# A fused attention and expert-routing kernel: a third buffer of token rows, another order of loads, and weight pieces held back at the seam

## The chip, the cores and the metric

One Trainium2 chip, one of its NeuronCores. The metric is the device time of one execution of the whole program in microseconds (us). TensorE (PE in the rows) multiplies matrices, VectorE (DVE) and ScalarE (ACT) work on elements, GpSimd (POOL) does some elementwise work and issues DMAs from its own queue, and SyncE (SP) only issues DMAs. The 16 DMA engines of the core serve both queues.

## What is computed

Linear attention with decay over blocks of 64 positions, and then a mixture of eight experts on its output, one expert per token:

```python
for b in range(nb):                                  # q, k, v: 4 batches, 8 heads, 768 positions, 64 wide, fp32
    intra = einsum('bhij,bhjd->bhid', (qb @ kb.T) * Dmask, vb)
    inter = einsum('bhid,bhde->bhie', qb * lam_pow, kv_state)
    out[:, :, sl] = intra + inter
    kv_state = lam_block * kv_state + einsum('bhsd,bhse->bhde', kb * rev_pow, vb)
x = out as 3072 rows (tokens) of 512
logits = normalised(x) @ normalised(expert_emb).T / tau      # 8 experts
e = argmax(logits); gate = softmax(logits)[e]
out[token] = gate * (max(x[token] @ w1[e], 0) @ w2[e])       # w1: 512x1024, w2: 1024x512 per expert, fp32 in memory
```

## The kernel before, in words

**Attention.** The 3072 tokens are 24 tiles of 128, six to a batch. The loop `for i in range(-2, R)` is a software pipeline with the order of every engine written out by hand: slot i loads k and v for tiles ahead (`load_k`, `load_v`, 256 KB each) and q for a pair of tiles ahead (`load_q`, 512 KB), transposes q and k of tile i + 2 (`pe_Tq` L302, `pe_Tk` L315), routes tile i - 1 (`pe_X`, L403), forms the scores of tile i + 1 (`pe_ST`, L327) and the output of tile i (`pe_O`, L363). ACT copies a pair of q into `qr` (`act_q`, L284), and `pe_Tq` waits for that. Pool scales k into `ks` (`pool_ks`). All q, k and v loads stand in SP's queue in program order, and a load waits there until its buffer is free: `qn` has 2, `kn` 4, `vn` 6.

**Routing.** `pe_X` leaves each token's row in `xg` (fp16 values, the token's number and its gate). Tiles are routed in groups: four groups of four tiles, four groups of two. The first tile of a group takes an `xg` buffer (`tensor_copy` L400 on DVE, with z, the scores and all later DVE work behind it); a buffer is free when all `scatter`s (L524, Pool) of the group that had it before have landed. Groups of four have 2 buffers, groups of two have 3. `scatter` writes a tile's rows to the expert's area of `xs_dram`; `at(i, "pool", ...)` fixes the slots, and `late` spreads a group's scatters over slots. Slots for weight pieces ("w") are a list of tile numbers. Pool's DMAs take turns on eight semaphores, and each waits until the DMA eight before it has landed.

**The seam.** Rows of an expert's area come in two parts: tiles below `TA` fill rows from 0, later tiles go on at row `CA` = 256 at the earliest (`bump`). So rows 0 to 255 of the first three experts (`NA`) can be read early (`load_early`): a one-element read `mark` of `xs_dram` (L552) waits for all scatters so far, and the three reads ("a", L546) follow it on SP. Scatters that come later in the program wait for `mark`, since it reads what they write. `early_xT` transposes the first of these row blocks in an attention slot. `fill` writes rows that are never used with an out-of-range number. After the loop come the last tile's routing, its two scatters, then the reads of the remaining rows: three "b" (L546), four small ones for the joint remainder (`x_q`, L565), and all 384 rows of expert 3 ("f", L546). PE meanwhile runs both layers (`pe_L1` L747, `pe_L2` L779) for the early rows A[0] to A[2], then B_[0] to B_[2], then experts 3 to 7 (F_[3] to F_[7]).

**Weights.** Each expert has four pieces (two of w1, two of w2), 512 KB each after the cast to fp16. `load_w` issues the next piece from Pool. Twelve go out in attention, two after it, and the other 18 behind the output writes: `put` (L760, L763) scales a block of output on DVE, writes it by an indirect DMA from Pool, and then issues `more.get(n_scat, 1)` pieces. Once, before F_[3], DVE waits for a Pool instruction that stands behind such a `put`: `overs` has Pool write `pstart` (an iota, L799), DVE computes `below` from it, and the copy `add_q` (L729) that completes F_[3]'s rows stands behind that on DVE.

Of the kernel before, what the change touches and what calls it, by code (L numbers as in the profile page):

```python
# [22 lines left out]
def kernel(  # L23
# [19 lines left out]
    R = B * RB  # L43
# [12 lines left out]


    NA = 3
    TA = 18
    CA, CE, GE = 256, 416, 3  # L60
    CQ = CE - GE * P
    NQ = P // CQ
# [49 lines left out]
    def load_q(j):  # L112

        if not 0 <= j < NJ:
            return
        b, c = divmod(2 * j, RB)
        qn[j] = ring.tile([P, H, 2, D], FP32, name="qn", tag="qn", bufs=2)
        nc.sync.dma_start(qn[j], q[b, :, ds(c * P, 2 * P), :].rearrange("h (p s) d -> p h s d", s=2))
# [8 lines left out]
    def load_v(i):  # L127
        if not 0 <= i < R:
            return
        b, c = divmod(i, RB)  # L130
        vn[i] = ring.tile([P, H, D], FP32, name="vn", tag="vn", bufs=6)
        nc.sync.dma_start(vn[i], v[b, :, ds(c * P, P), :].rearrange("h p d -> p h d"))

    load_k(0)
    load_q(0)
    load_k(1)
    load_v(0)
    nc.sync.dma_start(emb_sb, moe_expert_emb)
    load_k(2)
    load_q(1)  # L140
    load_k(3)
    load_v(1)

# [55 lines left out]
    nsq_all = const.tile([P, R], FP32, name="nsq_all")  # L199
    z_sb = const.tile([P, 2, 4, E], FP32, name="z_sb")  # L200
    ohcum = const.tile([P, E], FP16, name="ohcum")
    GZ = 6
    zrow = wk.tile([P, GZ, DM2], I32, name="zrow", tag="zrow", bufs=1)
    row_a = const.tile([P, 2], FP32, name="row_a")
    row_b = const.tile([P, 1], FP32, name="row_b")
# [186 lines left out]
    def xT_of(i, a):  # L392
        return xT[i][:, a // 2, a % 2, :]

    def pe_X(t):
        gi, j = group_of[t]
        if j == 0:
            nt = len(groups[gi])
            xg[gi] = xgp.tile([P, nt, DM2], I32, name="xg", tag=f"xg{nt}", bufs=2 if nt == 4 else 3)
            nc.vector.tensor_copy(xg[gi][:, 0:nt, DW : DW + 1],  # L400
                                  tok_iota[:, groups[gi][0] : groups[gi][0] + nt].unsqueeze(2))
        for a in range(DC):
            nc.tensor.matmul(xz[:, a // 2, a % 2, :], xT_of(t, a), ien[:, a, :], start=(a % 2 == 0),  # L403
                             stop=True, skip_group_check=True)
# [125 lines left out]

    def fill():

        p = P // 8
        rows = xs_dram.rearrange("(e r) d -> e r d", e=E)[:, CE - GZ * p : CE, :]
        nc.sync.dma_start(rows.rearrange("e (p g) d -> p e (g d)", p=p),
                          zrow[0:p].rearrange("p g d -> p (g d)").unsqueeze(1)
                          .to_broadcast([p, E, GZ * DM2]))


    xe, xi, xTe, xq, hT, hq = {}, {}, {}, {}, {}, {}  # L540
# [59 lines left out]
    def at(i, slot, fn, *a):  # L600
        todo.setdefault((i, slot), []).append((fn, a))
# [5 lines left out]
    for gi in range(GL):  # L607
        n = groups[gi][-1] + 1
        at(n, "z", rt_a, gi)
        at(n, "end", rt_n, gi)  # L610
        at(n + 1, "dve", rt_a2, gi)
        if groups[gi][0] == TA:
            at(n + 1, "pe", pe_part)
            at(n + 2, "dve", rt_part)
        at(n + 1, "pe", pe_rank, gi)
        if n + 2 < R:
            at(n + 2, "dve", rt_b, gi)
            at(n + 2, "z", rt_c, gi)
            at(n + 2, "end", rt_d, gi)
        else:  # L620
            at(n + 1, "pe", rt_b, gi)
            at(n + 1, "pe", rt_c, gi)
            at(n + 1, "mid", rt_d, gi)
            for j in range(2):
                at(n + 1, "mid", scatter, gi, j)
        if n + 2 < R:
            for j in range(len(groups[gi])):
                late = 0 if n >= TA else (j + 1) // 2 if n > TA - 4 else j
                at(min(n + 2 + late, R - 1), "pool", scatter, gi, j)
    at(0, "sp", fill)  # L630
    at(21, "sp", load_early)
    for i in (8, 11, 14, 16, 17, 18, 18, 19, 19, 22, 22, 22):
        at(i, "w", load_w, 1)

    def early_xT():
        xt_copy(("a", 0), 0, 2, ps.tile([P, DC * 2 * P], FP16, name="q_xtr", tag="q"))

    at(R - 1, "pe3", early_xT)

    act_q(0)  # L640
    pool_ks(0)
    for i in range(-2, R):
        if i >= -1:
            load_k(i + 5)
            load_v(i + 3 if i < 2 else i + 4)
            if i == 1:
                load_v(5)
            if i % 2 == 0:
                load_q(i // 2 + 2)
        run(i, "sp")  # L650
        pe_Tq(i + 2)
        pe_Tk(i + 2)
# [47 lines left out]
    ntile = const.tile([P, E], I32, name="ntile")  # L700
    pstart = const.tile([P, R], FP32, name="pstart")
    n_scat = [0]
    more = {2: 2, 3: 2, 9: 0, 10: 0, 11: 2, 12: 2}

    with (
        tc.tile_pool(name="wpool2", bufs=3) as wpool2,
# [47 lines left out]
        def put(y_ps, key, g):  # L754
# [14 lines left out]
                oob_is_err=False,  # L769
            )  # L770

            load_w(more.get(n_scat[0], 1))
            n_scat[0] += 1

        def pe_L2(key, g):
# [35 lines left out]

        A, B_, F_ = ([(k, e) for e in range(E)] for k in "abf")
        load_w(2)
        pe_X(R - 1)
        rt_a(GL)
        rt_a2(GL)
        rt_n(GL)
        pe_L1(A[0], range(4))
        pe_rank(GL)
        rt_b(GL)  # L820
        rt_c(GL)
# [149 lines left out]
```

## Time and profile before

| | |
|---|---|
| time, median of 3 runs | 285.45 us (284.69 to 287.54) |
| the profiled execution: time, span | 287.21 us, 285.3 us |
| busy share of the span: PE, DVE, ACT, POOL | 82%, 43%, 45%, 35% |
| mean granted TensorE clock | 0.924 of full |
| the chain that ended last: PE, DMA, issue, DVE, ACT | 44%, 20%, 11%, 8%, 8% |
| read from and written to HBM | 55.88 MB, 10.78 MB |

The span runs from the first to the last instruction; 1.9 us of the profiled execution lie around it. The share of the chain is what the last-ending sequence of waits and work was made of, and it changes along the span, so the stages are read apart.

### The profile page before, as it was taken

The page shows a single profiled execution, that of the slowest core. Times are in us where ns is not written, and L with a number is a line of the kernel's source. Part 1 is how long each engine was busy: PE and PEld are TensorE (multiplying, and loading weights), DVE is VectorE, ACT ScalarE, POOL GpSimd, SP SyncE. Part 2 cuts the span into 40 slices and gives each one's busy share as a digit, 9 for nine tenths or more (in the row PEclk, how much of TensorE's full clock was granted, in tenths as well). Part 3 has the DMA queues.
Part 4 walks back from the last instruction along what each step waited for, and adds up shares of the span by engine and source line. Part 5 has one row for each costly group of instructions (what it writes and reads, how often), then busy time and mean ns, then how long its engine had stood idle before and what let it go on. Part 6 is the DMA issues. An engine that isn't in the chain of part 4 may idle for free.

```text
span 285.3 us, 7195 instructions
## 1 busy us (share of the span) xinstructions
PE 233.3 (82%) x2926; PEld 176.3 (62%) x2926; DVE 123.6 (43%) x413; ACT 127.6 (45%) x282; POOL 101.1 (35%) x142
## 2 busy tenths in 40 slices
PE   0899669998399769989898797539949999999970
PEld 0688558887388658978777575216725465555520
DVE  1265325655445255676966322014531534334340
ACT  5765334662436155556435654004614353643500
POOL 4651211075009303905625655022420355132150
PEclk9999969999779979999999999658987999999995
DMA  7999989689709976997976999999982179960220
GB/s 159 237 243 150 208 200 197 140 212 191 184 22 196 202 177 137 206 211 154 215 159 157 178 241 268 251 268 285 196 162 40 65 168 230 256 195 38 77 106 18
DMA packets 72558, 49.93 MB, mean 175 GB/s; under 512 B 52024, under 2 KB 64952, under 8 KB 72515
## 3 DMA queue, kind: packets, MB, share of 16 engines
q0 software_dynamic: 7840, 26.25, 41.9%
q1 hardware_dynamic: 64674, 23.13, 36.3%
q8 instruction: 25, 0.41, 0.6%
q14 instruction: 19, 0.15, 0.2%
HBM read 55.88 MB, written 10.78 MB: 234 GB/s over the span
## 4 chain that ended last, share of the span: by engine, by line
PE 44%; DMA 20%; issue 11%; DVE 8%; ACT 8%; POOL 4%; SPq 2%; POOLq 1%; ACTq 0%; DVEq 0%
DMA xs_dram<-xg,si 9%; PE h_ps L747 7%; DMA qn<-in_q_dram 7%; PE s_ps L327 6%; PE y_ps L779 6%; PE o_ps L363 5%; PE xps L403 5%; DMA x_q<-xs_dram 5%; PE q_ps L302 4%; POOL out_dram L763 3%; PE o_ps L380 3%; PE k_ps L315 3%; PE o_ps L354 2%; ACT qr L284 2%; ACT xT L369 2%
## 5 line engine op out<-in xcount | busy, mean ns | idle before, releaser
L747 PE MATMUL h_ps<-xTe,w_sb 128*128 128x416 f16 (+2 forms) x352 | 51.4, 303 | 6.0 <-DVE xTe L729 3.8
L749 ACT ACTIVATE hT<-h_ps 128x384 f16<-128x384 f32 (+2 forms) x88 | 34.8, 402 | 41.4 <-PE h_ps L747 40.4
L763 POOL DMA_INDIRECT out_dram<-y_sb,xi x26 | 26.1, 1002 | 76.2 <-DVE y_sb L760 46.3
L747 PEld LDWEIGHTS <-w_sb 128*128 128x128 f16 x352 | 36.5, 116 | 21.1 <-issue 10.8
L524 POOL DMA_INDIRECT xs_dram<-xg,si x24 | 24.5, 1020 | 66.6 <-ACT kT L317 22.5
L779 PE MATMUL y_ps<-w_sb,hT 128*128 128x512 f16 x192 | 47.7, 400 | 0.0
L302 PE MATMUL q_ps<-ident,qr 128*128 128x128 f32 x96 | 18.0, 317 | 23.1 <-ACT qr L284 23.1
L290 POOL TENSOR_TENSOR ks<-kn,kdec 128x512 f32<-128x512 f32 x24 | 25.3, 1055 | 30.9 <-DMA kn<-in_k_dram 12.4
L336 DVE TENSOR_TENSOR stm<-s_ps,step 64x512 f32<-64x512 f32 (+1 forms) x48 | 30.7, 676 | 12.9 <-PE s_ps L327 12.9
L760 DVE TENSOR_SCALAR y_sb<-y_ps,x_e 128x512 f32<-128x512 f32 x24 | 18.0, 750 | 41.6 <-PE y_ps L779 39.1
L779 PEld LDWEIGHTS <-hT 128*128 128x128 f16 x192 | 18.9, 102 | 20.6 <-issue 3.3
L408 ACT ACTIVATE sq<-xps 128x512 f16<-128x512 f32 x24 | 14.3, 597 | 36.6 <-DVE z_sb L405 29.6
L403 PE MATMUL xps<-ien,xT 128*128 128x136 f32 x192 | 29.0, 298 | 1.6 <-ACT xT L369 1.6
L327 PE MATMUL s_ps<-qT,kT 64*64 64x64 f32 (+1 forms) x768 | 28.7, 270 | 1.2 <-DVE qT L304 0.8
L302 PEld LDWEIGHTS q_ps<-ident,qr 128*128 128x128 f32 x96 | 11.6, 157 | 27.6 <-ACT qr L284 17.0
L403 PEld LDWEIGHTS xps<-ien,xT 128*128 128x128 f32 x192 | 26.4, 207 | 2.4 <-ACT xT L369 2.2
L327 PEld LDWEIGHTS s_ps<-qT,kT 64*64 64x64 f32 x768 | 22.6, 143 | 5.2 <-DVE qT L304 2.4
L363 PE MATMUL o_ps<-stm,vn 128*64 128x128 f32 x384 | 25.3, 274 | 0.0
L751 DVE TENSOR_SCALAR hq<-h_ps 128x32 f16<-128x32 f32 x64 | 12.2, 191 | 27.2 <-ACT hT L749 26.1
L369 ACT COPY xT<-o_ps 128x512 f32<-128x512 f32 x24 | 14.0, 585 | 19.1 <-PE o_ps L363 19.0
L363 PEld LDWEIGHTS o_ps<-stm,vn 128*64 128x64 f32 x384 | 20.6, 137 | 0.7 <-issue 0.7
L304 DVE TENSOR_TENSOR qT<-q_ps,lamq 128x512 f32<-128x512 f32 x24 | 16.3, 679 | 9.9 <-PE q_ps L302 9.9
(126 smaller groups left out, 267.6 us busy)
## 6 DMA issues: line engine op xcount, KB each, us to landing
w_sb<-in_moe_w_dram POOLq DMA_DIRECT2D x32, 512.0 KB, 9.5
kn<-in_k_dram SPq DMA_DIRECT2D x24, 256.0 KB, 5.7
qn<-in_q_dram SPq DMA_DIRECT2D x12, 512.0 KB, 5.6
vn<-in_v_dram SPq DMA_DIRECT2D x24, 256.0 KB, 5.6
x_e<-xs_dram SPq DMA_DIRECT2D x5, 387.0 KB, 14.9
xs_dram<-zrow SPq DMA_DIRECT2D x1, 774.0 KB
x_e<-xs_dram SPq DMA_DIRECT2D x3, 258.0 KB, 3.1
out_dram<-y_sb,xi POOLq DMA_INDIRECT x26, 3.1
```

What stands on the lines that cost most here:

```text
L290: nc.gpsimd.tensor_tensor(ks[i], kn[i], kdec[:, i % RB].unsqueeze(2).to_broadcast([P, H, D]), op=ALU.mult)
L302: nc.tensor.transpose(t[:, hp, :], qr[j][:, s, 2 * hp : 2 * hp + 2, :].rearrange("p h d -> p (h d)"), ident)
L327: nc.tensor.matmul(sb[ds(C * c, C), h2, hp, c:2, :], kT[i][ds(64 * h2, 64), hp, ds(C * c, C)], q_of(i, hp, c)[ds(64 * h2, 64)], start=(hp ...
L336: nc.vector.tensor_tensor(stm[i][0:n, :, :, c], sb[0:n, :, :, c], step[0:n, c].rearrange("p s i -> p (s i)").unsqueeze(1).unsqueeze(1) .to ...
L363: nc.tensor.matmul(o_at(h2, u, b2), vn[i][:, 2 * hp + h2, :], stm[i][:, h2, hp], start=(i % RB == 0 and b2 == 0), stop=True, skip_group_ch ...
L369: nc.scalar.copy(xT[i].rearrange("p b h t -> p h b t"), bank["o"][:, :, 0 : 2 * P].rearrange("p h (b t) -> p h b t", t=P))
L403: nc.tensor.matmul(xz[:, a // 2, a % 2, :], xT_of(t, a), ien[:, a, :], start=(a % 2 == 0), stop=True, skip_group_check=True)
L524: nc.gpsimd.indirect_dma_start(out=xs_views[groups[gi][j]], out_offset=bass.IndirectOffsetOnAxis(ap=slot_i[gi][:, j : j + 1], axis=0), in_ ...
L747: nc.tensor.matmul(h_ps[:, 0:n], w_cols(w, c, fc), xTe[key][:, c, 0:n], start=(c == 0), stop=(c == DC - 1))
L749: nc.scalar.activation(hT[key][:, fc, 0:nm], h_ps[:, 0:nm], AF.Relu)
L763: nc.gpsimd.indirect_dma_start(out=out_views[n_scat[0]], out_offset=bass.IndirectOffsetOnAxis(ap=xi[key][:, g : g + 1], axis=0), in_=y[:], ...
L779: nc.tensor.matmul(y_ps, hT[key][:, fc, ds(P * g, P)], w[:, fc, :], start=(fc == 0), stop=(fc == FC - 1))
```

## The change

Eight edits. Groups of four tiles get a third `xg` buffer. `vn` goes from 6 buffers to 5, v is asked at i + 3 throughout, and q at pair i/2 + 3 in place of i/2 + 2 (pair 1 and pair 2 move up accordingly at the start). `TA` goes from 18 to 16, with `load_early` in slot 20 in place of 21, `early_xT` in slot 22 in place of 23, and the scatters of the fourth group in pairs. `fill` writes 627 KB in two DMAs instead of 774 KB in one. The pieces in attention move to other slots. After the loop no piece goes out behind the first output write; behind the second, Pool copies one element of expert 3's rows into `seen`, so it waits for that read, and issues four pieces; the following counts are redistributed (18 as before). ACT's cast of the last tile's rows (`x_cast`) moves behind the first chunk of A[0]'s first layer.

```diff
-    TA = 18
+    TA = 16
-        vn[i] = ring.tile([P, H, D], FP32, name="vn", tag="vn", bufs=6)
+        vn[i] = ring.tile([P, H, D], FP32, name="vn", tag="vn", bufs=5)
...
     load_k(1)
-    load_v(0)
+    load_q(1)
     nc.sync.dma_start(emb_sb, moe_expert_emb)
     load_k(2)
-    load_q(1)
+    load_v(0)
...
-            xg[gi] = xgp.tile([P, nt, DM2], I32, name="xg", tag=f"xg{nt}", bufs=2 if nt == 4 else 3)
+            xg[gi] = xgp.tile([P, nt, DM2], I32, name="xg", tag=f"xg{nt}", bufs=3)
...
+        for ne, p, end in ((NA, P // GZ // 4, CA), (E, P // GZ // 2, CE)):
+            rows = xs_dram.rearrange("(e r) d -> e r d", e=E)[0:ne, end - GZ * p : end, :]
...
-                late = 0 if n >= TA else (j + 1) // 2 if n > TA - 4 else j
+                late = 0 if n > TA else j // 2 if n == TA else j
     at(0, "sp", fill)
-    at(21, "sp", load_early)
-    for i in (8, 11, 14, 16, 17, 18, 18, 19, 19, 22, 22, 22):
+    at(20, "sp", load_early)
+    for i in (8, 10, 12, 14, 15, 16, 17, 20, 20, 21, 21, 22):
         at(i, "w", load_w, 1)
...
-    at(R - 1, "pe3", early_xT)
+    at(R - 2, "pe3", early_xT)
...
+            if i == -1:
+                load_q(2)
             load_k(i + 5)
-            load_v(i + 3 if i < 2 else i + 4)
-            if i == 1:
-                load_v(5)
+            load_v(i + 3)
             if i % 2 == 0:
-                load_q(i // 2 + 2)
+                load_q(i // 2 + 3)
...
-    more = {2: 2, 3: 2, 9: 0, 10: 0, 11: 2, 12: 2}
+    more = {1: 4, 2: 1, 3: 1, 4: 2, 5: 2, 6: 1, 7: 1, 8: 1, 9: 1, 11: 2, 12: 2}
...
-            load_w(more.get(n_scat[0], 1))
+            if n_scat[0] == 1:
+                nc.gpsimd.tensor_copy(seen, xe["f", NA][0:1, 0, DW : DW + 1])
+            load_w(more.get(n_scat[0], 0))
...
-        pe_X(R - 1)
+        pe_X(R - 1, cast=False)
         rt_a(GL)
         rt_a2(GL)
+        pe_L1(A[0], range(1))
+        x_cast(R - 1)
+        pe_L1(A[0], range(1, 2))
         rt_n(GL)
-        pe_L1(A[0], range(4))
+        pe_L1(A[0], range(2, 4))
```

On SP, from the v load of tile 2 to the q load of pair 3 (qn_428), before:

```order
L132 DMA vn_271<-in_v_dram 128x8x64
L118 DMA qn_273<-in_q_dram 128x8x128
L535 DMA xs_dram_78<-zrow_161 16x8x1548
L125 DMA kn_344<-in_k_dram 128x8x64
L132 DMA vn_346<-in_v_dram 128x8x64
L132 DMA vn_348<-in_v_dram 128x8x64
L125 DMA kn_424<-in_k_dram 128x8x64
L132 DMA vn_426<-in_v_dram 128x8x64
L118 DMA qn_428<-in_q_dram 128x8x128
```

On SP now, from the q load of pair 2 (qn_195) to `fill`, with pair 3 as qn_275:

```order
L118 DMA qn_195<-in_q_dram 128x8x128
L125 DMA kn_197<-in_k_dram 128x8x64
L132 DMA vn_199<-in_v_dram 128x8x64
L125 DMA kn_271<-in_k_dram 128x8x64
L132 DMA vn_273<-in_v_dram 128x8x64
L118 DMA qn_275<-in_q_dram 128x8x128
L540 DMA xs_dram_78<-zrow_161 8x3x1032
L540 DMA xs_dram_78<-zrow_161 16x8x1032
```

The q load of pair 3 moved from behind `fill` and five loads of k and v to just ahead of `fill`, with the third and fourth v load now behind it or close to it.

On Pool near the end of attention, before, from the scatter of tile 15 to those of tiles 20 and 21 (xg_1706 holds tiles 16 and 17, xg_1887 tiles 18 and 19):

```order
L524 DMA xs_dram_78<-xg_1354,si_1792 24576x258
L524 DMA xs_dram_78<-xg_1706,si_1976 24576x258 x2
L524 DMA xs_dram_78<-xg_1887,si_2155 24576x258 x2
L276 DMA w1_sb_1954<-in_moe_w1_dram 128x2048
L276 DMA w2_sb_1955<-in_moe_w2_dram 128x2048 x2
L524 DMA xs_dram_78<-xg_2085,si_2263 24576x258 x2
```

On Pool now, from the scatters of tiles 16 and 17 (xg_1711, the first that wait for `mark`) to those of tiles 18 and 19:

```order
L529 DMA xs_dram_78<-xg_1711,si_1987 24576x258 x2
L276 DMA w2_sb_1599<-in_moe_w2_dram 128x2048
L276 DMA w1_sb_2068<-in_moe_w1_dram 128x2048 x2
L276 DMA w2_sb_2069<-in_moe_w2_dram 128x2048
L529 DMA xs_dram_78<-xg_1887,si_2158 24576x258 x2
```

The first scatters behind `mark` were those of tiles 18 and 19 and are now those of tiles 16 and 17, with four weight pieces queued between them and the next scatters.

On Pool after the loop, before, from the last two pieces that go out without an output write to the second output write (y_sb_2489):

```order
L276 DMA w1_sb_2335<-in_moe_w1_dram 128x2048 x2
L524 DMA xs_dram_78<-xg_2243,si_2395 24576x258 x2
L763 DMA out_0_dram<-y_sb_2472,xi_2470 3072x512
L276 DMA w2_sb_2336<-in_moe_w2_dram 128x2048
L763 DMA out_0_dram<-y_sb_2489,xi_2470 3072x512
```

On Pool now, from the last tile's scatters to the third output write (y_sb_2575) and a piece behind it:

```order
L529 DMA xs_dram_78<-xg_2255,si_2397 24576x258 x2
L769 DMA out_0_dram<-y_sb_2474,xi_2472 3072x512
L769 DMA out_0_dram<-y_sb_2490,xi_2472 3072x512
L779 COPY seen_2318<-x_e_2448 1x1
L276 DMA w2_sb_2338<-in_moe_w2_dram 128x2048 x2
L276 DMA w1_sb_2498<-in_moe_w1_dram 128x2048 x2
L769 DMA out_0_dram<-y_sb_2575,xi_2573 3072x512
L276 DMA w2_sb_2499<-in_moe_w2_dram 128x2048
```

The pieces behind the first two output writes moved behind the copy that waits for expert 3's rows, and all later output writes and pieces stand behind that wait too.

## Rows read from the trace of the kernel before

**Rows 1.** Chain that ended last, in order of time: start us, us, what.

```profile
30.25 6.93 DMA qn<-in_q_dram
...
163.49 10.54 DMA xs_dram<-xg,si
...
197.11 1.74 PE y_ps L779 x8
```

**Rows 2.** Timeline of PE, output matmuls of tiles: start us, us, what.

```profile
32.19 1.05 PE L363 MATMUL o_ps<-stm,vn 128*64 128x128 f32 x16
...
44.95 1.05 PE L363 MATMUL o_ps<-stm,vn 128*64 128x128 f32 x16
...
64.24 1.05 PE L363 MATMUL o_ps<-stm,vn 128*64 128x128 f32 x16
...
70.47 1.04 PE L363 MATMUL o_ps<-stm,vn 128*64 128x128 f32 x16
...
82.52 1.05 PE L363 MATMUL o_ps<-stm,vn 128*64 128x128 f32 x16
...
96.84 1.05 PE L363 MATMUL o_ps<-stm,vn 128*64 128x128 f32 x16
...
107.90 1.04 PE L363 MATMUL o_ps<-stm,vn 128*64 128x128 f32 x16
...
153.25 1.09 PE L363 MATMUL o_ps<-stm,vn 128*64 128x128 f32 x16
```

**Rows 3.** Timeline, DVE taking an `xg` buffer; in brackets idle time and what ended it.

```profile
73.44 0.17 DVE L400 COPY xg<-tok_iota 128x4 int32<-128x4 int32 x1 [4.35 <-DMA xs_dram<-xg,si]
...
100.14 0.17 DVE L400 COPY xg<-tok_iota 128x4 int32<-128x4 int32 x1 [5.08 <-DMA xs_dram<-xg,si]
```

**Rows 4.** Windows: length, busy PE, PEld, DVE, ACT, POOL, then clock, DMA share, GB/s.

```profile
32.00:153.00 121.00, 102.39 (x1800) 90.64 (x1798) 67.33 (x216) 55.78 (x125) 42.22 (x45) 0.93 0.82 178
...
229.00:256.00 27.00, 27.00 (x161) 15.90 (x159) 9.88 (x33) 13.40 (x25) 11.08 (x15) 1.00 0.93 221
...
45.00:65.00 20.00, 19.92 (x376) 17.70 (x373) 12.51 (x38) 11.67 (x25) 6.96 (x7) 1.00 0.78 178
66.00:76.00 10.00, 4.74 (x97) 3.94 (x96) 4.43 (x10) 3.09 (x8) 2.16 (x3) 0.94 0.96 199
```

**Rows 5.** DMA issues of the page: KB each, median us to landing.

```profile
qn<-in_q_dram SPq DMA_DIRECT2D x12, 512.0 KB, 5.6
...
xs_dram<-xg,si POOLq DMA_INDIRECT x24, 5.7
```

**Rows 6.** Timeline, Pool, SP and DVE at the seam.

```profile
149.38 0.26 SPq L552 DMA_DIRECT2D mark<-xs_dram  x1
...
152.38 0.16 DVE L400 COPY xg<-tok_iota 128x2 int32<-128x2 int32 x1
...
159.06 1.16 POOL L276 DMA_DIRECT2D w_sb<-in_moe_w_dram  x2
...
167.63 0.58 POOL L276 DMA_DIRECT2D w_sb<-in_moe_w_dram  x1 [1.01 <-DMA w_sb<-in_moe_w_dram]
...
177.62 17.61 SPq L546 DMA_DIRECT2D x_e<-xs_dram  x4
```

**Rows 7.** Timeline of PE and Pool from A[2]'s first layer to F_[5]'s.

```profile
173.07 3.66 PE L747 MATMUL h_ps<-xTe,w_sb 128*128 128x256 f16 x32
...
181.44 0.61 PE L593 MATMUL xtr<-ident,x_e 128*128 128x128 f16 x4 [4.71 <-DMA x_e<-xs_dram]
...
193.88 3.01 PE L747 MATMUL h_ps<-xTe,w_sb 128*128 128x160 f16 x32
...
210.95 0.20 POOL L799 IOTA pstart<- 128x24 f32 x1
...
212.39 8.60 PE L747 MATMUL h_ps<-xTe,w_sb 128*128 128x416 f16 x32 [3.84 <-DVE xTe L729]
...
251.79 5.79 PE L747 MATMUL h_ps<-xTe,w_sb 128*128 128x416 f16 x32
```

More of the change, by code (lines that the diff above doesn't have):

```diff
@@ L201 @@
     ohcum = const.tile([P, E], FP16, name="ohcum")
-    GZ = 6
+    GZ = 4
     zrow = wk.tile([P, GZ, DM2], I32, name="zrow", tag="zrow", bufs=1)
@@ L393, in xT_of, with pe_X @@
         return xT[i][:, a // 2, a % 2, :]
-    def pe_X(t):
+    def pe_X(t, cast=True):
         gi, j = group_of[t]
@@ L408, in pe_X, with x_cast @@
         nc.scalar.activation(sq, xz[:, :, :, 0:P], AF.Square, accum_out=nsq_all[:, t : t + 1])
+        if cast:
+            x_cast(t)
+    def x_cast(t):
+        gi, j = group_of[t]
         nc.scalar.copy(
@@ L531, in fill @@
     def fill():
[L533 to L537, printed above, removed]
+        for ne, p, end in ((NA, P // GZ // 4, CA), (E, P // GZ // 2, CE)):
+            rows = xs_dram.rearrange("(e r) d -> e r d", e=E)[0:ne, end - GZ * p : end, :]
+            nc.sync.dma_start(rows.rearrange("e (p g) d -> p e (g d)", p=p),
+                              zrow[0:p].rearrange("p g d -> p (g d)").unsqueeze(1)
+                              .to_broadcast([p, ne, GZ * DM2]))
     xe, xi, xTe, xq, hT, hq = {}, {}, {}, {}, {}, {}
@@ L702 @@
     n_scat = [0]
-    more = {2: 2, 3: 2, 9: 0, 10: 0, 11: 2, 12: 2}
+    more = {1: 4, 2: 1, 3: 1, 4: 2, 5: 2, 6: 1, 7: 1, 8: 1, 9: 1, 11: 2, 12: 2}
+    seen = const.tile([1, 1], I32, name="seen")
     with (
```

## The prediction, on record before the changed kernel ran

> **What bounds the kernel now.** I read the chain that ended last first, in order of time, for its long DMA pieces. Three of those matter here: a q load in early attention (6.93 us), and at the seam a scatter that took 10.54 us to land [rows 1]. The timeline of PE then gives the pace. Undisturbed, four tiles take 64.24 - 44.95 = 19.29 us, so 4.82 each; at that pace the 20 steps from tile 3 to tile 23 would take 96.4, and they took 121.1 [rows 2]. Three steps hold most of the loss: tile 3 to 4 took 12.76 (7.9 too long), 9 to 10 took 12.05 (7.2), and 13 to 14 took 11.06 (6.2) [rows 2]. The first is the q load of pair 3, issued at 30.25 and landed at 37.18, when tile 4 should already have been at work [rows 1, 2]. The other two are DVE waiting, in front of all its later work, for an `xg` buffer whose last scatter had not landed [rows 3]. These losses include the stretch after each wait in which PE's granted clock was down (0.93 on average over 32 to 153 us, against 1.00 in an undisturbed stretch) [rows 4].
>
> After attention PE has the early rows of three experts to work on, up to 173.07 + 3.66 = 176.73. It then waits for the b rows and `x_q` and reaches B_[0]'s first layer only at 193.88 [rows 7]. What it waits for began with the last scatter: issued at 163.49, landed at 174.03 [rows 1], behind weight pieces in Pool's queue [rows 6]; the reads then share the DMA engines with more pieces. From there on PE waits once more, 3.84 us in front of F_[3] [rows 7], and is busy all of the time in the stretch that follows [rows 4].
>
> **The q load.** Pair 3 is now asked before `fill` and before five loads that stood in front of it. It and all that stands ahead of it are 4.7 MB; at the 178 GB/s of attention [rows 4] that is 26.5 us from the start. ACT wants it one tile ahead of tile 4, at about 32.2 [rows 2]. I count the whole 7.9. For later pairs the request comes four tiles (19.3 us) ahead of its use, against a median landing of 5.6 [rows 5]. v is asked when the same buffer comes free as before (tile i - 2, since both the depth and the buffers fell by one), still over four tiles ahead, so it costs nothing; if it came late each tile would wait by itself. `fill` writes 147 KB less, 0.7 us of DMA time at 221 GB/s [rows 4], in one more issue on SP; I count nothing for it.
>
> **The third buffer.** With three, the group of tiles 8 to 11 takes a fresh one, and that of tiles 12 to 15 waits for scatters that went out over five tiles earlier, 24 us against a median landing of 5.7 [rows 5]. Both waits go: 7.2 + 6.2 = 13.4. What is late next? A stretch without waits and without pieces ran at a DMA share of 0.78 with PE busy 19.92 of 20 us [rows 4]. A piece is 0.524 MB, 2.37 us at 221 GB/s [rows 4]. The change issues seven in ten tiles (48.2 us): 16.6 us of DMA time, a share of 0.34, so 1.12 in all. The backlog grows to about 6 us, or 9 if 0.93 is all that can be had. The loads have 19.3 - 5.6 = 13.7 us to spare, so I expect the backlog to stay behind that. Both parts together: -21.4.
>
> **`mark` one tile sooner.** The scatters of tiles 16 and 17 now wait for `mark`, and the `xg` buffer of the last group (two tiles, three buffers) waits for those two. Before, no scatter behind `mark` was asked for by a buffer, and the copy at 152.38 waited for nothing [rows 6]. `mark` was issued at 149.38 [rows 6]; one tile sooner is 144.6 on the same scale. Its landing and one scatter's (5.7 [rows 5]) put the buffer at about 153 to 156, so between no wait and one scatter's landing: 0 to +5.7. `early_xT` one tile sooner meets the same reads. I take +2, nearer to none, since the two issue points are close. Pool has no k tile left behind that wait (the last, tile 23, is issued ahead of it); the four pieces are.
>
> **The seam.** From the start of the last tile, t0 = 153.25 [rows 2], the second of the last scatters is issued at t0 + 10.2 in both. Seven pieces are ahead of it since `mark`, 16.6 us of DMA time from about t0 - 3, so it lands at about t0 + 15 (before: + 20.8) [rows 1, 2]. The issue of the reads up to the one of expert 3 takes 177.62 - 174.03 = 3.6 [rows 1, 6], and with no pieces in flight I give them 4 to land: t0 + 23. PE gets to `x_q` at 176.73 + 0.61 + 1.74 = t0 + 25.8 (four transposes, a block of the second layer [rows 1, 7]), so it waits for nothing. Of the 17.15 from 176.73 to 193.88 it then needs 2 x (0.61 + 1.74) = 4.7 [rows 1, 7]: -12.4, and down to -9.8 if the scatter lands no sooner than now. ACT's cast behind the first chunk takes at most its own 0.6 off the routing; I count nothing.
>
> **What the hold costs.** Pool's copy into `seen` waits for expert 3's rows, until t0 + 23. Behind it are all output writes from the third on, and `pstart`, for which DVE and then PE wait. DVE has six output blocks to write into, and four puts follow in that time, so PE is not stopped by them. But Pool may have eight DMAs under way, as the piece at 167.63 shows, which waited for an older piece [rows 6]. The ninth output write, ahead of `pstart`, so waits for the eighth piece after the release. Eight pieces at 2.37, three output writes of 0.262 MB at 1.2, and two reads of 0.396 MB at 1.8 make 26.2 us: t0 + 49. With that write, a piece, and 212.39 - 210.95 = 1.4 from `pstart` to PE [rows 7], F_[3] starts at about t0 + 52.5. Without a longer hold it would start at 193.88 - 12.4 + (212.39 - 193.88) = 200.0, t0 + 46.7. So +5.8 by this sum; 0 if the rows land 4 us sooner and the pieces take 2.1, 8 at the other end. I take +5. The slow start of F_[3] (8.60 against 5.79 [rows 7]) stays.
>
> **The sum.** -21.4 + 2 - 12.4 + 5 = -26.8 against the profiled execution's 287.21: 260.4. That execution lies 1.8 above the median, so against 285.45 it is **258.6 us**.
>
> **Rivals.** *The DMA engines become the bound in attention.* From 32 to 153 us they were busy 0.82 x 121 = 99.2 us, and the window of the first `xg` wait had a share of 0.96 while PE was busy less than half [rows 4]: part of that wait's time was used to catch up. If all of this work has to pass before attention ends, at 0.93 [rows 4] it takes 106.7, and 14.3 is gained for 21.4: 265.7. Against it: the last pieces need not land by then, and 0.78 suffices without pieces.
>
> The Trainium skill (DMA: Bandwidth & Descriptors, Issuing engines are not separate DMA queues) says that DMAs from every issuing queue run on the same 16 engines and interleave, so that asking elsewhere or sooner gives no more bandwidth; by that rule this rival holds and the time is 265.7. The trace agrees as far as the 0.96 goes, and no row shows whether the prefetch can carry the backlog.
>
> *The seam stays late.* Scatters land at t0 + 20.8 as now: `x_q` at t0 + 28.4, 2.6 too late for PE, and the hold ends 5.8 later, which F_[3] feels but for the 2.6: 258.6 + 5.8 = 264.4. For it: seven pieces since `mark` where there were five. Against it: four of these are issued before t0.
>
> *The hold makes it slower.* Each us by which expert 3's rows land after t0 + 23 delays all remaining pieces and F_[3]. It takes 26.8 to lose everything, so from t0 + 50 on the kernel is slower than before; at + 53 it is 288.5. The longest landing in these rows is 10.54, under far more traffic [rows 1], so I give it little.
>
> *The buffer isn't the limit, and q's order neither*, so that the same waits come back under other names: only the seam counts, 285.45 - 12.4 + 5 = 278.
>
> **Chances.** Forecast 0.55, DMA bound 0.23, late seam 0.13, waits under other names 0.04, slower 0.03, no net change 0.02. With both added waits at nothing the forecast reads 258.6 - 7 = 251.6; the rivals at 264.4 and 265.7, with the upper ends of the two waits (+ 3), reach 269. So 251 to 269 leaves out about 2 in 10. Within 1% is about what a measurement of this kernel cannot tell from no change: faster 0.95, same 0.02, slower 0.03.
>
> **What the profile will show.** Right: output matmuls of tiles 3 and 4, 9 and 10, 13 and 14 each about 4.8 apart; no idle time of DVE at its `xg` copies for groups of four; the last tile's output at about 132 to 135; `x_q` landed before PE asks, and L1 of B_[0] some 28 us after t0; a longer wait of DVE for `pstart` ahead of F_[3], with Pool's pieces waiting for pieces. Wrong: PE waiting for ACT's `qr` or Pool's `ks` with the DMA share above 0.9 all through tiles 10 to 20 (DMA bound); PE idle at `xtr_q` (late seam); an idle time of over 5 at the last `xg` copy; a `seen` later than t0 + 30.

## The result, and the profile after

The changed kernel takes 263.23 us (median of 4 runs, 262.32 to 265.82). The kernel before, on the same chip, takes 286.5 (284.69 to 290.03). The ratio is 0.922, 95% interval 0.912 to 0.933. Ratios and their intervals, here and below, leave out runs that fell in the chip's slower state; medians are of all runs. The prediction was 258.6, in a range of 251 to 269: the sign and the range held, the time is 4.6 us above the forecast, and 23.3 us are gained where 26.8 were forecast. The profiled execution is one of 263.92 us with a span of 262.0; the one before had 287.21 and 285.3, so 23.3 us are to be found between the two traces.

Timeline of PE of the changed kernel, output matmuls of tiles 3, 4, 8 to 10, 13, 14 and 23 (start us, us, what). They answer to [rows 2].

```profile
31.73 1.04 PE L363 MATMUL o_ps<-stm,vn 128*64 128x128 f32 x16
36.63 1.05 PE L363 MATMUL o_ps<-stm,vn 128*64 128x128 f32 x16
...
56.49 1.04 PE L363 MATMUL o_ps<-stm,vn 128*64 128x128 f32 x16
63.47 1.05 PE L363 MATMUL o_ps<-stm,vn 128*64 128x128 f32 x16
68.38 1.04 PE L363 MATMUL o_ps<-stm,vn 128*64 128x128 f32 x16
...
82.69 1.04 PE L363 MATMUL o_ps<-stm,vn 128*64 128x128 f32 x16
87.59 1.05 PE L363 MATMUL o_ps<-stm,vn 128*64 128x128 f32 x16
...
134.36 1.09 PE L363 MATMUL o_ps<-stm,vn 128*64 128x128 f32 x16
```

The three long steps are gone: tile 3 to 4 takes 4.90 (12.76 before), 9 to 10 takes 4.91 (12.05), 13 to 14 takes 4.90 (11.06). The last tile starts at t0 = 134.36, which was 153.25: **18.9 us** gained in attention. These are single executions: in experiment 5, which leaves the kernel before's attention as it was, the three long steps are still there (11.07, 8.92 and 11.83), but the last tile starts at 149.31, so that up to some 4 us of the 18.9 can be the execution's and not the change's. What is still long is the step from tile 8 to 9, 6.98, and it was 6.23 before.

At the seam, from SP's and Pool's timelines of the changed kernel (in brackets the idle time in front and what ended it); they answer to [rows 6]:

```profile
154.88 7.21 SPq L551 DMA_DIRECT2D x_e<-xs_dram  x4
```

```profile
143.82 0.99 POOL L529 DMA_INDIRECT xs_dram<-xg,si  x1 [0.30 <-ACT xTe L600]
...
159.18 0.18 POOL L779 COPY seen<-x_e 1x1 int32<-1x1 int32 x1 [10.95 <-DMA x_e<-xs_dram]
159.42 2.20 POOL L276 DMA_DIRECT2D w_sb<-in_moe_w_dram  x4
...
175.80 1.03 POOL L769 DMA_INDIRECT out_dram<-y_sb,xi  x1 [4.37 <-DMA w_sb<-in_moe_w_dram]
...
187.47 1.03 POOL L769 DMA_INDIRECT out_dram<-y_sb,xi  x1 [2.48 <-DMA out_dram<-y_sb,xi]
188.49 0.56 POOL L276 DMA_DIRECT2D w_sb<-in_moe_w_dram  x1
189.03 0.20 POOL L807 IOTA pstart<- 128x24 f32 x1
```

And PE over the same stretch, which answers to [rows 7]:

```profile
158.84 0.39 PE L727 MATMUL xtr_q<-ident,x_q 128*128 128x128 f16 x4
159.07 1.89 PE L787 MATMUL y_ps<-w_sb,hT 128*128 128x512 f16 x8
160.79 2.85 PE L753 MATMUL h_ps<-xTe,w_sb 128*128 128x160 f16 x32
...
174.91 0.39 PE L598 MATMUL xtr<-ident,x_e 128*128 128x128 f16 x4
190.46 7.47 PE L753 MATMUL h_ps<-xTe,w_sb 128*128 128x416 f16 x32 [15.16 <-DVE xTe L735]
```

In the kernel before, PE stood at this place:

```profile
190.09 0.58 PE L721 MATMUL xtr_q<-ident,x_q 128*128 128x128 f16 x4 [4.63 <-DMA x_q<-xs_dram]
```

Now PE goes through `x_q` without a wait, and B_[0] starts at t0 + 26.4 where it was t0 + 40.6: **14.2** gained. But in front of F_[3] PE now stands for 15.16 us where it stood for 3.84, and F_[3] starts at t0 + 56.1 where it was t0 + 59.1. From B_[0] to F_[3] it took 18.51 and takes 29.67: **11.2** lost. From F_[3] to the end 1.4 are gained, most of it in F_[3]'s first layer (7.47 for 8.60). The account closes: -18.9 - 14.2 + 11.2 - 1.4 = -23.3.

The chain that ended last, in order of time, names the last scatter's landing and what fills those 15 us:

```profile
143.82 7.69 DMA xs_dram<-xg,si
...
159.42 1.29 POOL w_sb L276 x3
161.06 13.96 DMA w_sb<-in_moe_w_dram
175.05 0.75 issue
175.80 1.00 POOL out_dram L769
176.80 12.95 DMA w_sb<-in_moe_w_dram
189.80 11.38 issue
```

The fourth piece behind `seen` takes 13.96 us to land; Pool's sixth output write, eight DMAs behind it, waits for it. All this stands in Pool's queue ahead of `pstart`, a row of constants that takes 0.20 us to make. DVE wants it before it copies expert 3's last tokens:

```profile
178.57 0.16 DVE L589 TENSOR_TENSOR xi<-x_e,m 128x1 int32<-128x1 int32 x1 [5.01 <-DMA out_dram<-y_sb,xi]
...
189.27 0.36 DVE L813 TENSOR_TENSOR below<-over,pstart 128x192 f32<-128x192 f32 x1 [9.53 <-POOL pstart L807]
```

Two waits stand there one behind the other. The first (5.01) is for an `xi` buffer, which an output write still holds that was issued behind pieces; the second (9.53) is for `pstart`.

Windows of the changed kernel (columns as in [rows 4]):

```profile
32.00:132.00 100.00, 94.03 (x1770) 82.56 (x1765) 66.53 (x204) 54.43 (x122) 42.38 (x46) 1.00 0.95 209
...
175.50:190.50 15.00, 0.04 (x1) 0.07 (x2) 2.11 (x9) 0.42 (x1) 7.04 (x10) 0.66 1.06 240
```

In attention the DMA share rose from 0.82 to 0.95 with PE busy 94 of 100 us: a share near one, and PE's few waits there end with steps of DVE and ACT, none with a load. (Pool waits three times for a k load, 7.0 us in all.) In the second window PE does nothing while the DMA engines are full.

### The profile page after: what moved, and what is told of

It reads as the page before. It is cut to its first block, busy times and chain, and to the rows that moved or that the text cites. A ratio compares the mean times of both kernels' runs of the same rounds, so it can differ in the third digit from the quotient of the medians.

```text
span 262.0 us, 7196 instructions
## 1 busy us (share of the span) xinstructions
PE 221.4 (84%) x2926; PEld 168.3 (64%) x2926; DVE 124.6 (48%) x413; ACT 127.6 (49%) x282; POOL 100.9 (39%) x143
## 4 chain that ended last, share of the span: by engine, by line
PE 33%; DMA 21%; issue 19%; DVE 10%; ACT 6%; POOL 6%; SPq 1%; POOLq 1%; DVEq 0%
DMA w_sb<-in_moe_w_dram 13%; PE s_ps L327 7%; PE o_ps L363 7%; DMA xs_dram<-xg,si 5%; PE xps L403 5%; POOL out_dram L769 5%; PE o_ps L380 4%; PE q_ps L302 3%; PE o_ps L354 3%; PE k_ps L315 2%; ACT xT L369 2%; DVE qT L304 2%; DMA qn<-in_q_dram 2%; DMA x_e<-xs_dram 2%; ACT qr L284 1%
## 5 line engine op out<-in xcount | busy, mean ns | idle before, releaser
L753 PE MATMUL h_ps<-xTe,w_sb 128*128 128x416 f16 (+2 forms) x352 | 50.3, 298 | 16.2 <-DVE xTe L735 15.2
L753 PEld LDWEIGHTS <-w_sb 128*128 128x128 f16 x352 | 36.1, 114 | 30.3 <-issue 19.4
L769 POOL DMA_INDIRECT out_dram<-y_sb,xi x26 | 26.2, 1007 | 56.6 <-DVE y_sb L766 34.5
L787 PE MATMUL y_ps<-w_sb,hT 128*128 128x512 f16 x192 | 44.2, 379 | 0.0
L787 PEld LDWEIGHTS <-hT 128*128 128x128 f16 x192 | 18.0, 98 | 18.7
L408 ACT ACTIVATE sq<-xps 128x512 f16<-128x512 f32 x24 | 14.3, 597 | 28.0 <-DVE z_sb L405 18.3
L403 PE MATMUL xps<-ien,xT 128*128 128x136 f32 x192 | 26.6, 281 | 1.6 <-ACT xT L369 1.4
L327 PE MATMUL s_ps<-qT,kT 64*64 64x128 f32 (+1 forms) x768 | 26.8, 259 | 0.3
L403 PEld LDWEIGHTS xps<-ien,xT 128*128 128x128 f32 x192 | 23.9, 190 | 2.4 <-ACT xT L369 2.2
L302 PE MATMUL q_ps<-ident,qr 128*128 128x128 f32 x96 | 16.7, 299 | 9.2 <-ACT qr L284 9.2
L327 PEld LDWEIGHTS s_ps<-qT,kT 64*64 64x64 f32 x768 | 21.0, 135 | 4.1 <-DVE qT L304 1.7
L276 POOL DMA_DIRECT2D w_sb<-in_moe_w_dram x32 | 18.1, 577 | 9.1 <-DMA w_sb<-in_moe_w_dram 6.6
```

The costliest lines, as they stand in the source:

```text
L302: nc.tensor.transpose(t[:, hp, :], qr[j][:, s, 2 * hp : 2 * hp + 2, :].rearrange("p h d -> p (h d)"), ident)
L327: nc.tensor.matmul(sb[ds(C * c, C), h2, hp, c:2, :], kT[i][ds(64 * h2, 64), hp, ds(C * c, C)], q_of(i, hp, c)[ds(64 * h2, 64)], start=(hp ...
L753: nc.tensor.matmul(h_ps[:, 0:n], w_cols(w, c, fc), xTe[key][:, c, 0:n], start=(c == 0), stop=(c == DC - 1))
L769: nc.gpsimd.indirect_dma_start(out=out_views[n_scat[0]], out_offset=bass.IndirectOffsetOnAxis(ap=xi[key][:, g : g + 1], axis=0), in_=y[:], ...
L787: nc.tensor.matmul(y_ps, hT[key][:, fc, ds(P * g, P)], w[:, fc, :], start=(fc == 0), stop=(fc == FC - 1))
```

## Experiments

Each is timed against the kernel before on the same chip, three rounds each (the last five). Experiments 7, 10 and 11 ran on a second chip and 12 on a third, so a few us between these sets are read from the ratios and not from the times.

**1. The place of `pstart`, on the changed kernel.**

```
+    nc.gpsimd.iota(pstart, ...)        # at the start of the expert stage
 ...
 def overs():
-    nc.gpsimd.iota(pstart, ...)
```

> The changed kernel, with Pool's `pstart` row made at the start of the expert stage instead of behind Pool's output writes and pieces. Theory A (the place in Pool's queue): only `pstart` held F_[3] back, everything else it needs was there. DVE's mask for the last b rows still ends at 178.6, so F_[3]'s first layer starts at about 180 instead of 190.5, and the kernel takes 263.2 - 10.4 = about 253. Theory B (the weights): the DMA engines were busy at 0.99 in front of F_[3], the pieces for F_[3]'s second layer and for F_[4] land no sooner than before, and PE's wait only moves behind F_[3]'s start: 260 to 264.

Measured: 253.22, ratio 0.888 (0.882 to 0.893), 10.0 less than the changed kernel. F_[3] starts at 181.37 (t0 + 47.8), after a wait of 6.80. Theory A holds: one small instruction's place in Pool's queue made 8.4 of the 15.16 us, and the weights were there. The 6.80 that are left are the first of the two waits, for an `xi` buffer, which had lain hidden under the second. From PE's and DVE's timelines of this kernel:

```profile
181.37 7.30 PE L755 MATMUL h_ps<-xTe,w_sb 128*128 128x416 f16 x32 [6.80 <-DVE xTe L737]
```

```profile
179.11 0.16 DVE L589 TENSOR_TENSOR xi<-x_e,m 128x1 int32<-128x1 int32 x1 [6.27 <-DMA out_dram<-y_sb,xi]
```

**2. The same with eight `xi` buffers.**

```
-        xi[key] = rsm.tile([P, GE], I32, name="xi", tag="xi", bufs=4)
+        xi[key] = rsm.tile([P, GE], I32, name="xi", tag="xi", bufs=8)
```

> As the first of these, and eight buffers for `xi` instead of four, so that the mask of the last b rows waits for no output write (5.0 us at 178.57 in the changed kernel). Theory A: F_[3] starts at about 175.5, when B_[2] is done: 263.2 - 15 = about 248. Theory B (the output writes behind the pieces land late, or weights do): no better than the first.

Measured: 250.22, ratio 0.880 (0.872 to 0.888). From PE's timeline of this kernel:

```profile
174.51 0.39 PE L598 MATMUL xtr<-ident,x_e 128*128 128x128 f16 x4
176.93 5.79 PE L755 MATMUL h_ps<-xTe,w_sb 128*128 128x416 f16 x32 [2.03 <-DVE xTe L737]
```

F_[3] starts at t0 + 43.0, 13.1 sooner than in the changed kernel, and its first layer takes 5.79 in place of 7.47: the granted clock over it is 1.00, and 0.77 in the changed kernel, where PE had stood for 15 us. The window from 177 to 237 us has PE busy 60.00 of 60.00. The gain is 13 against the 15 expected; the 2.03 that are left end with DVE, which scales an output block and works out the overflow (`overs`) first.

**3. Without the hold.**

```
-    more = {1: 4, 2: 1, 3: 1, 4: 2, 5: 2, 6: 1, 7: 1, 8: 1, 9: 1, 11: 2, 12: 2}
+    more = {2: 2, 3: 2, 9: 0, 10: 0, 11: 2, 12: 2}
 ...
-            if n_scat[0] == 1:
-                nc.gpsimd.tensor_copy(seen, xe["f", NA][0:1, 0, DW : DW + 1])
-            load_w(more.get(n_scat[0], 0))
+            load_w(more.get(n_scat[0], 1))
```

> The changed kernel without the copy into `seen`; pieces follow the output writes by the table of the kernel before. Theory A: the hold costs the 11.2 us by which F_[3] starts later after B_[0] than it did, and the seam's gain of 14.2 comes in large part from scatters and reads that no pieces compete with. Without it the seam loses 5 to 10 and F_[3] gains 11: 258 to 263. Theory B: the seam's gain came from the earlier scatters alone, so the hold buys nothing: 252 to 253. Theory C: the hold buys more than it costs: 266 or above.

Measured: 263.19, ratio 0.924 (0.918 to 0.930), the same time as with the hold (263.23). Theories B and C fall, and A stands at its upper end. PE's timeline of this kernel, with t0 = 133.41:

```profile
158.05 0.40 PE L598 MATMUL xtr<-ident,x_e 128*128 128x128 f16 x4 [1.94 <-DMA x_e<-xs_dram]
...
166.47 0.58 PE L726 MATMUL xtr_q<-ident,x_q 128*128 128x128 f16 x4 [4.85 <-DMA x_q<-xs_dram]
...
170.27 3.52 PE L752 MATMUL h_ps<-xTe,w_sb 128*128 128x160 f16 x32
...
189.29 7.45 PE L752 MATMUL h_ps<-xTe,w_sb 128*128 128x416 f16 x32 [3.84 <-DVE xTe L734]
```

B_[0] starts at t0 + 36.9, 10.4 later than with the hold, because PE waits for the b rows and `x_q` again (1.94 and 4.85) and does the work right behind these waits at a low granted clock (0.50 from 166.40 to 170.20; the eight matmuls of a second layer there take 3.62, with the hold 1.89); F_[3] starts at t0 + 55.9 after the old wait of 3.84, and with the hold it is t0 + 56.1. So the hold (the copy, and the table of pieces that goes with it) moves the same 10 us from in front of B_[0] to in front of F_[3]. It supplies 10.4 of the seam's 14.2; 3.8 come from the rest of the change. Experiment 9 rules out q, v and the buffer for these; with the hold in place, the pieces' tiles in attention are worth 1.7 at B_[0] (experiment 10) and the sooner early reads 1.2 (experiment 11). ACT's later cast wasn't tested alone.

**4. Without the hold, `pstart` first, eight `xi` buffers** (the edits of 1 to 3 together).

> The changed kernel without the copy into `seen`, with `pstart` first and eight buffers for `xi`. Theory A (the hold's gain at the seam is real and was only hidden behind `pstart`): B_[0] starts 10 us later after the last tile than with the hold, and nothing comes back at F_[3] but its wait of 3.84 and 1.7 of slow start: 263.2 - 5.5 = about 258, some 8 slower than the same kernel with the hold (250.2). Theory B (the hold is worth nothing in any order): 250 to 252.

Measured: 259.94, ratio 0.912 (0.906 to 0.917), 9.7 more than experiment 2 (9.0 by the ratios), which differs by the hold alone. Theory A holds: the hold is worth its 10 us as soon as nothing wanted stands behind it in the queue. PE waits 1.50 and 5.93 at the seam here, and B_[0] starts at t0 + 36.1.

**5. `pstart` first, on the kernel before** (the edit of 1).

> The kernel before, with `pstart` made at the start of the expert stage. Theory A: the wait of 3.84 in front of F_[3] goes, and perhaps part of the slow start of F_[3] (8.60 against 5.79): 3.8 to 6.6 less, ratio 0.977 to 0.987. Theory B (weights or reads are next): no change that can be measured.

Measured: 282.47, ratio 0.989 (0.984 to 0.993); 2.7 gained. Theory B falls. In the trace F_[3] still waits 2.08 for DVE's own steps, and its first layer takes 7.47: 1.8 of the wait and 1.1 of the slow start are gone, 2.9 together, which is less than theory A's lower end of 3.8 (the interval, 2 to 4.5 us, doesn't rule that out). The place was worth little until the hold made it dear.

**6. The sooner q alone, on the kernel before.**

```
     load_k(1)
-    load_v(0)
+    load_q(1)
 ...
-    load_q(1)
+    load_v(0)
 ...
+            if i == -1:
+                load_q(2)
 ...
-                load_q(i // 2 + 2)
+                load_q(i // 2 + 3)
```

> The kernel before with the sooner q requests alone (q of pair 1 ahead of v of tile 0, each later q one pair sooner). Theory A (each wait is a loss of its own): the 7.9 us between tiles 3 and 4 go, and the two `xg` waits stay: 277. Theory B (DMA engines bound the stretch): an earlier q only puts another load later, 0 to 4 us gained: 281 to 285. If the `xg` waits lengthen because the tiles ahead come sooner, the gain ends at the first of them: also 281 to 285, but with the step from tile 3 to 4 at 4.9 and a longer idle time at DVE's second `xg` copy.

Measured: 282.52, ratio 0.987 (0.979 to 0.995). Tile 4 starts at 39.26 (44.95 before): 5.7 sooner, not 7.9, since tile 3 now comes late (34.36, 32.19 before). Timelines of Pool and of DVE in this kernel:

```profile
31.22 1.04 POOL L290 TENSOR_TENSOR ks<-kn,kdec 128x512 f32<-128x512 f32 x1 [8.00 <-DMA kn<-in_k_dram]
```

```profile
67.55 0.17 DVE L400 COPY xg<-tok_iota 128x4 int32<-128x4 int32 x1 [3.86 <-DMA xs_dram<-xg,si]
...
94.09 0.17 DVE L400 COPY xg<-tok_iota 128x4 int32<-128x4 int32 x1 [4.90 <-DMA xs_dram<-xg,si]
```

A k load has become the late one, and both `xg` waits stand as they were [rows 3]. So theory A has the mechanism, each wait a loss of its own (the last tile starts at 147.31, 5.9 sooner), but not the size: the time is in the range of theory B.

**7. v alone, on the kernel before.**

```
-        vn[i] = ring.tile([P, H, D], FP32, name="vn", tag="vn", bufs=6)
+        vn[i] = ring.tile([P, H, D], FP32, name="vn", tag="vn", bufs=5)
 ...
-            load_v(i + 3 if i < 2 else i + 4)
-            if i == 1:
-                load_v(5)
+            load_v(i + 3)
```

> The kernel before with v alone changed: five buffers in place of six, each v from tile 5 on asked for one tile later, q's order and `xg` as they were. Theory A (SP's queue: q of pair 3 stood behind two v requests that took 4.85 us to issue): that is what freed it in the kernel with the third buffer, so the step from tile 3 to 4 falls from 12.8 to about 6, both `xg` waits stay, and 5 to 7 are gained: 279 to 281. Theory B (the sooner q or the smaller `fill` did it): the step stays at 12.8 and the time at 285.

Measured: 284.77, ratio 0.994 (0.990 to 0.998). Tile 4 starts at 40.30, so 4.65 sooner, and the step to it takes 8.15. q of pair 3 is issued at 27.86 instead of 30.25, with q's order untouched: one v request fewer stands ahead of it on SP. Theory A has the place right and the size too large: the step falls to 8, not to 6. The `xg` waits stay (4.07 and 5.40). Only 1.6 is gained in the time, where theory A had 5 to 7. (The last tile starts at 149.21 in this trace, and at 149.31 in that of experiment 5, where attention wasn't edited at all; there tile 4 starts at 43.38.)

**8. The third `xg` buffer, on the kernel before,** with the edit of 7 and the smaller `fill`, which make room for it.

```
-    GZ = 6
+    GZ = 4
 ...
-            xg[gi] = xgp.tile([P, nt, DM2], I32, name="xg", tag=f"xg{nt}", bufs=2 if nt == 4 else 3)
+            xg[gi] = xgp.tile([P, nt, DM2], I32, name="xg", tag=f"xg{nt}", bufs=3)
```

> The kernel before with the third `xg` buffer alone, and what makes room for it (v in five buffers and asked later, `fill` in smaller rows). Theory A: both DVE waits go, 7.2 + 6.2 = 13.4: 271 to 272, and the step from tile 3 to 4 still takes 12.8. Theory B (DMA bound): waits return under other names, less than 6 gained: above 279.

Measured: 266.83, ratio 0.934 (0.927 to 0.940): 18.7 gained, more than theory A's 13.4. DVE's `xg` copies wait for nothing:

```profile
62.07 0.17 DVE L400 COPY xg<-tok_iota 128x4 int32<-128x4 int32 x1
80.97 0.17 DVE L400 COPY xg<-tok_iota 128x4 int32<-128x4 int32 x1
```

The last tile starts at 133.04, 20.2 sooner than before, and 16.2 sooner than with v alone. The step from tile 3 to 4 takes 5.92, not the 12.8 expected of it: v's part had moved q too, which I had not seen.

**9. q, v and the buffer, on the kernel before** (6 and 8 together).

> Both parts on the kernel before, with its pieces, its 18 early tiles and its seam. Theory A: their gains add up to 21.3, so that the last tile starts at about 132 and the kernel takes 264 to 266, all that the whole change gains, since hold and seam were found to cancel. Theory B: the sum of the two single gains is not reached by 4 or more, because the DMA engines have less idle time left: 268 or above.

Measured: 266.72, ratio 0.935 (0.929 to 0.941); the last tile starts at 132.33. Neither theory has it whole. The sum of parts, 21, is there in attention (20.9), but on top of the buffer's part the sooner q gives 0.7 us there and nothing in the time. B_[0] starts at t0 + 40.8, as in the kernel before. The whole change takes 3.5 less than this kernel, where nothing was expected beyond the parts in attention.

**10. Attention's pieces at their old tiles, on the kernel of experiment 2.**

```
-    for i in (8, 10, 12, 14, 15, 16, 17, 20, 20, 21, 21, 22):
+    for i in (8, 11, 14, 16, 17, 18, 18, 19, 19, 22, 22, 22):
```

> The fastest so far (the changed kernel with `pstart` first and eight `xi` buffers, 250.2), with the twelve pieces of attention issued at the tiles of the kernel before. Theory A (the earlier pieces cost what the changed kernel's tiles lack against the kernel before with both attention parts): the last tile starts 1.5 to 2 sooner, five pieces in place of seven lie between `mark` and the last scatter, so `x_q` comes no later, and 1.5 to 2.5 are gained: 248 to 249. Theory B (the pieces are wanted as early as they are): PE waits for weights in the expert stage, 251 or more.

Measured: 254.48, ratio 0.889 (0.884 to 0.894): 4.3 slower than experiment 2, or 2.5 by the ratios, whose intervals overlap, so the traces have to say what is slower. Theory A was wrong: the last tile starts at 134.04 against 133.93, so the earlier pieces cost attention nothing. They are worth something at the seam. Pool gives out five pieces just ahead of the last scatters here, and its timeline shows what that makes of the hold:

```profile
135.53 1.68 POOL L276 DMA_DIRECT2D w_sb<-in_moe_w_dram  x3
...
139.98 1.18 POOL L276 DMA_DIRECT2D w_sb<-in_moe_w_dram  x2
...
143.72 1.00 POOL L529 DMA_INDIRECT xs_dram<-xg,si  x1 [0.52 <-ACT xTe L600]
...
161.94 0.18 POOL L781 COPY seen<-x_e 1x1 int32<-1x1 int32 x1 [12.06 <-DMA x_e<-xs_dram]
```

The release comes at t0 + 27.9; in experiment 2 it came at t0 + 22.6 (156.56). F_[3] starts at t0 + 46.3 in place of + 43.0. Theory B has the sign and not the reason: PE waits 0.4, 0.9, 3.7 and 1.1 us from 150 us on (for the b rows, for `x_q`, at F_[3] and at F_[4]), and none of these waits ends with a piece. The last two end with DVE, which had stood 2.87 and 3.14 for output writes that stand behind the later release.

**11. 18 early tiles, on the kernel of experiment 2.**

```
-    TA = 16
+    TA = 18
-                late = 0 if n > TA else j // 2 if n == TA else j
+                late = 0 if n >= TA else (j + 1) // 2 if n > TA - 4 else j
-    at(20, "sp", load_early)
+    at(21, "sp", load_early)
-    at(R - 2, "pe3", early_xT)
+    at(R - 1, "pe3", early_xT)
```

> The fastest so far with the early reads of the kernel before: they cover 18 tiles, `mark` and the early transposes come one tile later. Theory A (the sooner `mark` is a part of the seam's gain: without the hold B_[0] started 3.8 sooner after the last tile than before): expert 0's early rows and with them the whole seam come later, 2 to 4 lost: 252 to 254. Theory B (the hold alone carries the seam's gain): no change that can be measured, 249 to 251.

Measured: 248.73, ratio 0.870 (0.864 to 0.876). Theory A falls: with the hold, the sooner early reads gain nothing in the time. The last tile starts 2.2 sooner (131.71), and B_[0] at t0 + 27.7 where it was t0 + 26.5. The difference to experiment 2, 1.5 in the time and 2.9 by the ratios, is within what the two intervals allow.

**12. `overs()` behind `add_q(F_[3])`, on the kernel of experiment 11.**

```
-        overs()
         pe_xT(F_[3], 2, 3)
         add_q(F_[3])
+        overs()
```

> The last kernel (18 early tiles, `pstart` first, eight `xi` buffers, 248.7) with `overs()` behind `add_q(F_[3])` in the program, so that DVE copies expert 3's last tokens before it works out the overflow. Theory A: DVE's six small steps (174.39 to 175.59 there, 1.2 us) go from in front of F_[3], which then waits only for ACT's copy (ends at 174.5) and starts 1.1 sooner; PE has no wait of over 1 us left between the last tile and the end, so nothing gives it back: 247.6, about the least that a measurement here can tell. Theory B: the weights of expert 4 or Pool's output writes are next, and nothing changes: 248.7.

Measured: 251.25, ratio 0.878 (0.873 to 0.884). PE's wait at F_[3] falls from 2.01 to 0.81, as theory A has it, but the kernel isn't faster: in this execution the last tile starts at 135.15, 3.4 later, though nothing ahead of it was edited. Attention differs by that much between executions of the same code (the kernel before and experiment 5 are 3.9 apart), so 1.2 us at F_[3] can't be told by the time, and kernels 2, 11 and 12 can't be ranked. All three beat the changed kernel by 12 to 14.5 us.

## Why the prediction was right, and where it was off

**Attention, -21.4 + 2 forecast, -18.9 measured.** The mechanism was right, and that the sum agrees to 0.5 is partly luck, as executions of the kernel before differ by some 4 us there: the three long steps were waits of their own, and the load stayed behind the prefetch. By experiment 9 the q load, v and the buffer together give -20.9 where -21.4 was forecast. The split was not right. "v costs nothing" missed that v's requests were what kept q of pair 3 back: v alone brings tile 4 forward by 4.65, q alone by 5.7, both with the buffer by 8.4 (44.95 to 36.55), which is less than the two added up, so a part of it is the same work. (From the 43.38 of experiment 5 it is 3.1, 4.1 and 6.8, and the overlap is small.) The buffer, with the smaller `fill`, gives 16.2 on top of v, not 13.4 (17 by the ratios of experiments 7 and 8). `fill` itself writes 165 KB less, not 147: the 627 KB are counted in 1000 bytes and the 774 KB in 1024. It is 0.75 us of DMA time and changes nothing here.

**`mark` one tile sooner, +2.** Neither the reason nor the size is borne out. Neither copy into the last groups' `xg` buffers waits for anything in the changed kernel. With 18 tiles the last tile starts 2.2 sooner in experiment 11, and 1.2 later in experiment 12, so no cost of `mark` can be told from what executions differ by. What makes 2.0 between experiment 9 and the changed kernel stays open.

**The seam, -12.4 forecast, -14.2 measured.** The scatter landed at t0 + 17.2 (143.82 + 7.69; forecast + 15), the rows of expert 3 at t0 + 24.8 (forecast + 23), and PE was at `x_q` at t0 + 24.5 (forecast + 25.8) and waited for nothing. That is the forecast's own mechanism, and experiment 3 shows that 10.4 of it hang on no pieces being in flight.

**The hold, +5 forecast, +11.2 measured: this is the term that was mis-sized.** The mechanism was as written: output writes and pieces ahead of `pstart`, each waiting for an older DMA. The release came at t0 + 24.8 instead of + 23 (1.8); from it to the ninth write it took 28.3 (159.18 to 187.47) instead of 26.2 (2.1), less 0.3 from there to PE; PE was ready 1.8 sooner than I had it, which only made the wait longer; and I had taken 5 where the sum said 5.8 (0.8). 5 + 1.8 + 2.1 - 0.3 + 1.8 + 0.8 = 11.2. The upper end of 8 was too low for a row of waits that all run the same way: whatever PE gains ahead of a fixed time in Pool's queue is lost there. What the prediction did not see is the wait for an `xi` buffer in front of the one for `pstart`: by itself, with DVE's steps behind it, it holds F_[3] until t0 + 47.8 (experiment 1), and it came out only when `pstart` was moved.

**The sum.** Against the forecast the trace is 0.5 worse in attention and 6.2 at the hold, and better by 1.8 at the seam and by 1.4 behind F_[3], where the slow start was to stay: 3.5, the difference between 26.8 and 23.3. That the seam and F_[3] made good half of the hold's error is luck.

**The rivals.** *DMA bound:* its sign was to be PE waiting with a share above 0.9; the share was 0.95, and PE did not wait. Its time (265.7) lies closer to the result than the forecast does, by chance: it allowed attention to gain 14.3, and the parts in attention alone gain 18.8 in the time (experiment 9). The Trainium skill (DMA: Bandwidth & Descriptors, Issuing engines are not separate DMA queues) says that the engines are shared whoever issues. The seam agrees: in experiment 3, with pieces in flight, PE could use the `x_q` rows asked for from 152.65 only at 166.47, and with the hold those asked for from 153.02 at 158.84. The section is about which engine issues; that asking sooner gains nothing, as the prediction reads it, it does not say, and here a sooner request brought tile 4 forward (experiment 6). *Late seam:* B_[0] would have come at t0 + 31; it came at + 26.4. *Slower, no change, waits under other names:* the last one took place in part, though not where I had put it. The `xg` and q waits did not come back; the one removed at `x_q` did, at `pstart`.

## What to carry to other kernels

When a wait is put into an engine's queue, list every instruction behind it and ask of each who wants it and when: here a 0.2 us row of constants stood there and cost the 10 us that the wait had gained, and moving it in front got them back. A wait that goes from one place and turns up at the next at the same absolute time says that the time is set elsewhere; the hold is worth nothing with `pstart` behind it (263.2 with and without) and 9.7 with `pstart` in front and eight `xi` buffers (259.9 against 250.2). Parts of a change that free the same load are not to be added up: test them singly and together. And read a gain of a few us in one stage from more than one trace: here two executions of the same attention differ by 3.9.

## What the runs showed of the hardware

SP's queue has a pace of its own. In early attention single requests take from 0.4 to 5.1 us to issue, so that a request's place in the queue sets its time: one v fewer ahead of it brought the q of pair 3 forward by 2.4 us (30.25 to 27.86). What holds SP there wasn't tested.

A DMA share of 0.93 to 0.98 from 32 to 132 us went with PE busy 94 to 96 of 100 us at a granted clock of 1.00 in six kernels (the changed one, and experiments 2 and 8 to 11); the share alone doesn't tell that DMA is the bound.

DVE's steps are now and then six to ten times as long as their kind. These are Pool and DVE of the changed kernel at the step from tile 8 to 9:

```profile
60.96 1.06 POOL L290 TENSOR_TENSOR ks<-kn,kdec 128x512 f32<-128x512 f32 x1
```

```profile
60.25 1.83 DVE L442 TENSOR_TENSOR oh<-ohr,ohm 128x32 f16<-128x32 f32 x1
```

The median of this DVE instruction is 0.18. It ends at 62.08, Pool's at 62.02. Two more such pairs are in this trace (DVE's L438 at 101.08, 1.09 long, with Pool's `ks` ending 0.06 ahead of it; L507 at 116.97, 1.64 long, with 0.03), and PE waits 1.63 for the first. The Trainium skill (SBUF — State Buffer, SBUF: two separate sides) describes a port pair that GpSimd and VectorE, in an instruction with two SBUF inputs or in a mode that uses both ports, hold one at a time, for the whole instruction and whichever starts first. The ends that coincide agree with that. But the DVE steps at 60.25 and 116.97 start 0.71 and 0.56 ahead of Pool's `ks`, while Pool is still issuing a scatter, so by that rule Pool would have to hold the pair through the scatter too. No run here tested it.
